# Two small projections of a token mixer from one matmul, with one part turned by an identity matmul and the other copied by DMA

## The chip, the core and the metric

The kernel runs on one core of one Trainium2 chip. A core has a matrix engine (PE, or TensorE), a vector engine (DVE), a scalar engine (ACT), a general engine (POOL, or GpSimd) and a queue engine (SP, or SyncE), and 16 DMA engines move data for it. The metric is the device time of one execution in microseconds (us), lower is better. Seven executions of the kernel before took 113.78 to 116.05 us, with a median of 114.7 us.

## The reference, cut to what matters

There are 4 batches, 8 heads, 768 tokens and 64 values per head; a head's 768 tokens are 8 blocks of 96. An 8x8 matrix P per head, made nearly doubly stochastic, mixes the blocks of k and of v. Attention then runs inside each block. Its output x (768 x 512 per batch) goes through a token mixer and a last matrix.

```python
k_sorted = einsum('bhij,bhjcd->bhicd', P, k_b);  v_sorted = einsum('bhij,bhjcd->bhicd', P, v_b)
attn = softmax(scale * q_b @ k_sb^T)          # inside each block of 96
x = attn @ v_sb                               # as (batch, 768, 512)
wq = x @ w_q;  wk = x @ w_k                   # 512 -> 64 each
W_tok = scale * einsum('bsd,btd->bst', wq, wk)
mixed = einsum('bst,btd->bsd', W_tok, x)
out = maximum(mixed, 0) @ w_out
```

The kernel computes mixed as wq times (wk transposed times x), so the 768 x 768 matrix is never made. For wk transposed times x it needs wk with tokens on partitions; for the product with wq it needs wq with its 64 values on partitions.

## The kernel before, in words

The program is a hand-written order of small units, the string ORDER (line 21). Each unit is named by kind, batch and number; a letter says which engine empties its PSUM tile (a for ACT, d for DVE), and a number after that asks for so many filler matmuls ahead of it (line 84: 256 columns of ones, which compute nothing that is used). Every engine works through its own instructions in this order. So PE does its matmuls exactly as ORDER lists them, and a unit whose data is late holds up all that stands behind it. The units, per batch:

- Q (line 202, 4 of them): q turned by identity matmuls. K (line 223, 4): k mixed by P and turned. V (line 237, 4): v mixed by P.
- T (line 247, 8): a DMA that regroups v by blocks, from VS to VT, on SP's queue; in batch 0 every second one goes on POOL's.
- S (line 255, 8): the scores of a block, then the exponential E on ACT. AV (line 269, 8): E times v, then reciprocal R and product X on DVE.
- XT (line 288, 4): two blocks of x turned, giving XT with the 512 features on partitions.
- WQ (line 300, 2): 4 matmuls over 384 tokens, giving wq transposed. The weight tile wqd holds w_q twice side by side, so that wq transposed stands on partitions 0 to 63 and again on 64 to 127.
- WK (line 310, 2): wk with tokens on partitions, 4 blocks with 4 accumulating matmuls each, so 16 matmuls of 64 columns. XT is the stationary operand.
- A (line 323, 1): wk transposed times x. MIX (line 336, 4): A times wq, with relu. The two halves of A stand on partitions 0 to 63 and 64 to 127, which is why wq is needed on both.
- OUT (line 353, 6): 4 matmuls of 512 columns with w_out, a copy on ACT or DVE, and a DMA to the output; for batch 3 on SP's queue, else on POOL's.

PSUM has 3 two-bank slots, in which K, V, S, AV and MIX take turns, and 2 one-bank slots, in which Q, XT, WQ, WK, A and OUT take turns. A unit waits until the unit that held its slot has been emptied.

The inputs are loaded by POOL's queue, in the order q0, v0, k0, q1 at the start, and then, in further_loads (line 180), after the regroups of batch 0: v1, w_q, w_k, k1, w_out, q2, v2, k2, q3, v3, k3. These DMAs turn fp32 into bf16. Between them POOL makes the mixing matrices M of batches 1 and 2 (line 217) and copies w_q into the second half of wqd (line 188), for which it waits until w_q has landed.

Of the kernel before, what the change touches and what calls it, by code (L numbers as in the profile page):

```python
# [10 lines left out]
FP32 = mybir.dt.float32  # L11
BF16 = mybir.dt.bfloat16
# [6 lines left out]


ORDER = """
    V00d3 V01a V02d V03a K01d K02a T00 K03a T04 K00d T03 T01 T02 T07 Q12d10 Q13a T06 S00a T05
    S01a S02a Q11d Q10d AV00d AV01d AV02d S03a S05a XT00d AV03d S04a S07a S06a AV04d XT01a V12d
    V11a AV07d WK00a WQ00a AV05d AV06d V13a K13a XT02d K11a K12d K10a XT03d V10a S13a1 S14a WQ01d
    T10 WK01d T12 S17a S12a T11 S11a A00d T14 T16 S16a Q23d Q21d T13 MIX02a MIX01d T17 Q20a Q22d
    T15 MIX03a MIX00d S10a OUT05a5 AV10d OUT02a AV11d AV12d AV14d OUT01a XT10a V20a V21d OUT03a
    V23a AV17d V22a OUT04d AV16d AV13d OUT00a T26 T25 K22a T24 K23d XT13a T22 S15a Q31d T23 K21a
    Q30d T21 K20d Q32a T27 AV15d XT11a T20 S24a2 S20a Q33d S21a WK10d V30d V33a WQ10a V31a AV24d
    V32a XT12d S22a AV21d T30 S23a WQ11a T32 AV22d AV20d T31 AV23d WK11a T35 K32a T36 A10a1 K30a
    K31d K33a T37 T33 T34 XT21d XT20a MIX13d MIX12a S34a WK20d3 WQ20a S31a S32a MIX11d OUT15d  # L30
    AV31d OUT13a AV32d OUT14a AV34d MIX10a S30a S33a S25a OUT10d OUT12a AV33d AV25d OUT11a AV30d
    XT31a S35a XT22d S26a XT30d1 S27a AV35d AV26d WK30a AV27d XT32a S36a WQ30d S37a XT23d AV36d
    AV37d2 WQ21a WK21a XT33d A20a WQ31a WK31d MIX20a MIX21d MIX22a A30a MIX23a OUT22a OUT21a
    MIX33d MIX30a MIX32a OUT25d OUT23a MIX31d OUT35a OUT34a OUT32a OUT30a OUT33a OUT31a OUT20a
    OUT24a
"""
SLOTS = {"b": 3, "s": 2}

# [2 lines left out]
def kernel(  # L41
# [22 lines left out]
    DH = moe_w_q.shape[1]  # L64
    PT = DM // P
# [16 lines left out]
    def filler(t):  # L82
        while fill[0] > 0:
            nc.tensor.matmul(t, idb, ones[:, 0:256], start=True, stop=True, skip_group_check=True)
            fill[0] -= 1

    def psum(shape, dtype=FP32):
        t = psp.tile(shape, dtype, tag="ps", name="ps", bufs=SLOTS["b"])
        filler(t[:, 0, 0:256])
        return t  # L90

    def psum1(n, dtype=FP32):
        t = psp.tile([P, 512], FP32, tag="ps1", name="ps1", bufs=SLOTS["s"])
        filler(t[:, 0:256])
        return (t if dtype == FP32 else t.bitcast(dtype))[:, 0:n]


    Pm = const.tile([BH, NB + 1, NB], FP32)
    nc.sync.dma_start(out=Pm[:, 0:NB, :], in_=sort_net.rearrange("b h i j -> (b h) i j"))

    Qn, Kn, Vn = [None] * B, [None] * B, [None] * B

    def load_q(b):
        Qn[b] = inp.tile([P, H, R6, D], BF16, tag="Qn", name="Qn", bufs=3)
        nc.gpsimd.dma_start(out=Qn[b].rearrange("p h r d -> p h (r d)"),
                            in_=q[b].rearrange("h (p r) d -> p h (r d)", p=P))

    def load_k(b):
# [11 lines left out]
    idb = const.tile([P, P], BF16)  # L120
# [48 lines left out]

    nc.gpsimd.tensor_copy(L_j, m_j.unsqueeze(2).to_broadcast([P, NB, SP]))  # L170
    load_q(1)
    wqd = const.tile([P, PT, 2, DH], BF16)
    wk_t = const.tile([P, PT, DH], BF16)
    wo_t = const.tile([P, PT, DM], BF16)
    nc.gpsimd.memset(VS[0][:, :, :, D:D1], 1.0)
    nc.gpsimd.memset(VS[1][:, :, :, D:D1], 1.0)
# [1 line left out]
        nc.gpsimd.memset(KTs[n][:, NP * S:], 0.0)  # L178

    def further_loads():  # L180
        load_v(1)
        make_m(1, PTR, nc.gpsimd)
        nc.gpsimd.dma_start(out=wqd[:, :, 0, :], in_=moe_w_q.rearrange("(t p) d -> p t d", p=P))
        nc.gpsimd.dma_start(out=wk_t, in_=moe_w_k.rearrange("(t p) d -> p t d", p=P))
        load_k(1)
        nc.gpsimd.dma_start(out=wo_t, in_=moe_w_out.rearrange("(t p) d -> p t d", p=P))
        load_q(2)
        nc.gpsimd.tensor_copy(wqd[:, :, 1, :], wqd[:, :, 0, :])
        make_m(2, PTR, nc.gpsimd)
        load_v(2)  # L190
        load_k(2)
        load_q(3)
        load_v(3)
        load_k(3)


    Xb, XT, QT, KT, VT, Ms, Es = {}, {}, {}, {}, {}, {}, {}
    wqT, wkb, Ab, mixT, ts = {}, {}, {}, {}, {}
    hf = S // 2
    copies = {"ACT": nc.scalar.copy, "DVE": nc.vector.tensor_copy}  # L200

# [11 lines left out]
    def make_m(b, src, eng, parts=1):  # L213
        M = rot.tile([P, H, SP, NB], BF16, tag="M", name="M", bufs=3)
        n = H // parts
        for h in range(0, H, n):
            eng.tensor_mul(  # L217
                M[:, h:h + n],
                src[:, b * H + h:b * H + h + n].unsqueeze(2).to_broadcast([P, n, SP, NB]),
                m_s.unsqueeze(1).unsqueeze(3).to_broadcast([P, n, SP, NB]))  # L220
        Ms[b] = M
# [76 lines left out]
        copies[eng](XT[b][:, :, 2 * j * BLK:(2 * j + 2) * BLK], ps)  # L298

    def u_WQ(b, h, eng):  # L300
        if b not in wqT:
            wqT[b] = rot.tile([P, S], BF16, tag="wqT", name="wqT")
        ps = psum1(hf)
        for pt in range(PT):
            nc.tensor.matmul(ps, wqd[:, pt].rearrange("p a d -> p (a d)"),
                             XT[b][:, pt, h * hf:(h + 1) * hf],
                             start=(pt == 0), stop=(pt == PT - 1), skip_group_check=True)
        copies[eng](wqT[b][:, h * hf:(h + 1) * hf], ps)

    def u_WK(b, h, eng):  # L310
        if b not in wkb:
            wkb[b] = rot.tile([BLK, NB, DH], BF16, tag="wkb", name="wkb")
        n = NB // 2
        ps = psum1(n * DH).rearrange("p (i d) -> p i d", i=n)
        for ii in range(n):
            i = h * n + ii
            m = P if ii < n - 1 else BLK
            for pt in range(PT):
                nc.tensor.matmul(ps[0:m, ii, :], XT[b][:, pt, i * BLK:i * BLK + m], wk_t[:, pt, :],
                                 start=(pt == 0), stop=(pt == PT - 1), skip_group_check=True)  # L320
        copies[eng](wkb[b][:, h * n:(h + 1) * n], ps[0:BLK])

    def u_A(b, n, eng):
        ps = psum1(DM // 2)
# [11 lines left out]
    def u_MIX(b, n, eng):  # L336
        if b not in mixT:
            mixT[b] = rot.tile([P, PT, R6, P], BF16, tag="mixT", name="mixT")
        wqv = wqT[b].rearrange("p (i r s) -> p r i s", i=NB, r=R6)
        rh, p2 = n // 2, n % 2  # L340
        nr = R6 // 2
        ps = psum([P, 2, 512])
        for a in range(2):
            nc.tensor.matmul(ps[:, a, 0:hf], Ab[b][a * DH:(a + 1) * DH, p2 * P:(p2 + 1) * P],  # L344
                             wqv[a * DH:(a + 1) * DH, rh * nr:(rh + 1) * nr],
                             start=True, stop=True, skip_group_check=True)
        ov = mixT[b].rearrange("p (a t) r n -> p a t (r n)", a=2)[:, :, p2, rh * hf:(rh + 1) * hf]
        if eng == "ACT":
            nc.scalar.activation(ov, ps[:, :, 0:hf], ACT.Relu)  # L349
        else:  # L350
            nc.vector.tensor_relu(ov, ps[:, :, 0:hf])  # L351
# [45 lines left out]


    emit = {"Q": u_Q, "K": u_K, "V": u_V, "T": u_T, "S": u_S, "AV": u_AV, "XT": u_XT,
            "WQ": u_WQ, "WK": u_WK, "A": u_A, "MIX": u_MIX, "OUT": u_OUT}  # L400
    for kind, b, n, eng, m in re.findall(r"([A-Z]+)(\d)(\d)([ad]?)(\d*)", ORDER):
        b, n, fill[0] = int(b), int(n), int(m or 0)
        if (kind, b, n) == ("S", 1, 0):
# [33 lines left out]
```

The softmax here doesn't subtract the row's maximum and nothing guards it: scores larger than these inputs give would overflow.

## Time and profile before

| what | value |
|---|---|
| median of 7 executions | 114.7 us (113.78 to 116.05) |
| the profiled execution's own time | 113.68 us |
| its span, first to last instruction | 111.9 us |
| mean granted PE clock | 0.969 of full speed |
| PE busy | 93.4 us (83%), 1444 matmuls |
| ACT, DVE, POOL busy | 75.5, 68.8, 33.4 us |
| DMA | 19.80 MB, mean 177 GB/s |

The busy time of an engine is a sum over stages that have different limits, so what bounds a stage is read from that stage. Matmuls are pipelined: the duration of one holds its latency, and what a unit really costs in a dense stretch is the time from its first matmul's start to the start of the next unit's. The profile's line numbers are those of the kernel before.

### The profile page before, as it was taken

How to read it: one execution, taken by the hardware profiler on the slowest of the kernel's cores; microseconds unless marked ns; L12 is line 12 of the kernel's file. 1: busy time of each engine (PE TensorE's matmuls, PEld its weight loads, DVE VectorE, ACT ScalarE, POOL GpSimd, SP SyncE). 2: the span in 40 equal slices, each digit the busy share in tenths (PEclk: the TensorE clock that was granted, in tenths of full speed). 3: DMA queues.
4: the chain of work that ended last, by engine and by line, in shares of the span. 5: the costliest groups of instructions: out<-in, count | busy, mean ns of one | idle time of the engine just before them, and what ended most of it. 6: DMA issues, size and time to landing. Idle time of an engine off the chain costs nothing.

```text
span 111.9 us, 3418 instructions
## 1 busy us (share of the span) xinstructions
PE 93.4 (83%) x1444; PEld 62.8 (56%) x1444; DVE 68.8 (62%) x154; ACT 75.5 (67%) x116; POOL 33.4 (30%) x54
## 2 busy tenths in 40 slices
PE   0007899978698999999999999999899999999930
PEld 0007345866575766666588688655478686334400
DVE  1686768579365734878898776858488874071000
ACT  4014538587836998849599986995968836885640
POOL 6950000999089910041310000003150000051030
PEclk9999999998559999999999999999999999999999
DMA  0999999789999999999999999602543000048772
GB/s 3 110 202 205 203 203 199 204 156 181 161 200 205 205 204 220 246 236 207 203 212 247 250 362 367 176 2 94 192 171 120 0 0 6 0 164 304 292 269 95
DMA packets 19758, 19.80 MB, mean 177 GB/s; under 512 B 2208, under 2 KB 17696, under 8 KB 19744
## 3 DMA queue, kind: packets, MB, share of 16 engines
q0 software_dynamic: 15696, 15.21, 72.9%
q1 hardware_dynamic: 4048, 4.38, 12.9%
q8 instruction: 11, 0.18, 0.6%
q14 instruction: 3, 0.02, 0.1%
HBM read 20.19 MB, written 6.29 MB: 237 GB/s over the span
## 4 chain that ended last, share of the span: by engine, by line
issue 41%; DMA 28%; POOL 14%; DVE 9%; PE 2%; ACT 1%; POOLq 1%; ACTq 0%
DMA Vn<-in_v_dram 22%; DMA wqd<-in_moe_w_q_dram 6%; POOL out_dram L362 5%; POOL Vn L115 2%; POOL M L217 2%; POOL VT L252 2%; DVE M L217 1%; DVE tmp L162 1%; DVE Pm L161 1%; ACT Pm L155 1%; DVE tmp L163 1%; DVE tmp L160 1%; DVE tmp L159 1%; PE ps L366 1%; DVE VS L244 1%
## 5 line engine op out<-in xcount | busy, mean ns | idle before, releaser
L362 POOL DMA_DIRECT2D out_dram<-ot x18 | 9.8, 546 | 59.3 <-ACT ot L360 35.1
L265 ACT ACTIVATE E<-ps 96x768 bf16<-96x768 f32 x32 | 24.0, 810 | 1.4 <-PE ps L260 1.3
L357 PE MATMUL ps<-wo_t,mixT 128*128 128x512 bf16 x96 | 23.1, 379 | 0.0
L284 DVE TENSOR_TENSOR X<-ps,R 96x512 bf16<-96x512 f32 x32 | 22.0, 686 | 1.1
L360 ACT COPY ot<-ps 128x512 f32<-128x512 f32 x20 | 11.8, 588 | 9.1 <-PE ps L357 9.0
L206 PE MATMUL ps<-idb,Qn 128*64 128x128 bf16 x192 | 8.9, 244 | 9.0 <-DMA Qn<-in_q_dram 8.7
L277 PEld LDWEIGHTS <-E 96*128 96x128 bf16 (+1 forms) x256 | 11.8, 104 | 4.9 <-ACT E L265 2.0
L277 PE MATMUL ps<-VT,E 96*128 96x65 bf16 (+1 forms) x256 | 13.3, 199 | 0.8 <-ACT E L265 0.7
L357 PEld LDWEIGHTS <-mixT 128*128 128x128 bf16 x96 | 8.6, 98 | 9.3 <-issue 0.9
L206 PEld LDWEIGHTS <-Qn 128*64 128x64 bf16 x192 | 7.0, 124 | 10.1 <-DMA Qn<-in_q_dram 8.7
L260 PE MATMUL ps<-QT,KT 64*128 64x96 bf16 x256 | 10.0, 210 | 1.4 <-DVE X L284 0.8
L244 ACT CAST VS<-ps 128x768 bf16<-128x768 f32 x11 | 8.8, 829 | 2.0 <-PE ps L241 2.0
L283 DVE RECIPROCAL R<-ps 96x8 f32<-96x8 f32 x32 | 6.3, 198 | 5.9 <-PE ps L277 5.8
L260 PEld LDWEIGHTS <-KT 64*128 64x128 bf16 x256 | 7.0, 97 | 4.5 <-issue 1.6
L351 DVE TENSOR_SCALAR mixT<-ps 128x768 bf16<-128x768 f32 x7 | 6.7, 954 | 4.0 <-PE ps L344 3.9
L241 PE MATMUL ps<-Vn,M 128*128 128x384 bf16 x32 | 8.4, 370 | 0.8 <-DMA Vn<-in_v_dram 0.8
L234 ACT CAST KT<-ps 128x768 bf16<-128x768 f32 x10 | 7.8, 800 | 1.1 <-PE ps L230 1.0
L294 PE MATMUL ps<-idb,X 96*128 96x96 bf16 x128 | 8.3, 211 | 0.0
L230 PE MATMUL ps<-M,Kn 128*64 128x128 bf16 x192 | 7.4, 220 | 1.0 <-DVE R L283 0.5
L349 ACT ACTIVATE mixT<-ps 128x768 bf16<-128x768 f32 x9 | 7.1, 815 | 0.5 <-PE ps L344 0.5
L230 PEld LDWEIGHTS <-Kn 128*64 128x64 bf16 x192 | 6.0, 109 | 2.6 <-issue 1.5
L211 ACT COPY QT<-ps 128x768 bf16<-128x768 bf16 x7 | 5.5, 793 | 2.8 <-PE ps L206 2.8
(71 smaller groups left out, 130.3 us busy)
## 6 DMA issues: line engine op xcount, KB each, us to landing
out_dram<-ot POOLq DMA_DIRECT2D x18, 256.0 KB, 2.6
Qn<-in_q_dram POOLq DMA_DIRECT2D x4, 768.0 KB, 14.5
Vn<-in_v_dram POOLq DMA_DIRECT2D x4, 768.0 KB, 11.9
Kn<-in_k_dram POOLq DMA_DIRECT2D x4, 768.0 KB, 14.8
VT<-VS SPq DMA_DIRECT2D x28, 97.5 KB, 5.5
out_dram<-ot SPq DMA_DIRECT2D x6, 256.0 KB, 2.0
wo_t<-in_moe_w_out_dram POOLq DMA_DIRECT2D x1, 512.0 KB, 11.3
VT<-VS POOLq DMA_DIRECT2D x4, 97.5 KB, 3.1
```

Source lines behind the costliest of these rows:

```text
L206: nc.tensor.matmul(ps[hh * D:(hh + 1) * D, r, :], Qn[b][:, 2 * kp + hh, r, :], idb, is_transpose=True, start=True, stop=True, skip_group_c ...
L230: nc.tensor.matmul(ps[hh * D:(hh + 1) * D, r * P:(r + 1) * P], Kn[b][:, h, r, :], Ms[b][:, h].rearrange("p s i -> p (s i)"), start=True, s ...
L241: nc.tensor.matmul(ps[:, hh, 0:R6 * D], Ms[b][:, h].rearrange("p s i -> p (s i)"), Vn[b][:, h].rearrange("p r d -> p (r d)"), start=True, ...
L244: copies[eng](VS[b % 2][:, :, 2 * kp:2 * kp + 2, 0:D].rearrange("p r h d -> p h r d"), ps[:, :, 0:R6 * D].rearrange("p h (r d) -> p h r d" ...
L260: nc.tensor.matmul(ps[:, hh, kp * BLK:(kp + 1) * BLK], KT[b][hh * D:(hh + 1) * D, k0:k0 + P], QT[b][hh * D:(hh + 1) * D, kp, :, i * SP:(i ...
L265: nc.scalar.activation(E.rearrange("p (a n) -> p a n", a=2), ps[0:BLK, :, 0:4 * BLK], ACT.Exp, scale=scale)
L277: nc.tensor.matmul(ps[0:m, h // 4, (h % 4) * D1:(h % 4 + 1) * D1], E[:, e * BLK:e * BLK + m], VT[b][:, i, h, :], start=True, stop=True, sk ...
L284: nc.vector.tensor_mul(Xb[b][:, i].rearrange("p (a t d) -> p a t d", a=2, t=4), pv[:, :, :, 0:D], Rt.unsqueeze(3).to_broadcast([BLK, 2, 4, ...
L294: nc.tensor.matmul(ps[:, pt, ii * BLK:(ii + 1) * BLK], Xb[b][:, 2 * j + ii, pt * P:(pt + 1) * P], idb[0:BLK, 0:BLK], is_transpose=True, st ...
L357: nc.tensor.matmul(ps, mixT[b][:, pt, r, :], wo_t[:, pt, :], start=(pt == 0), stop=(pt == PT - 1), skip_group_check=True)
L360: copies[eng](ot, ps)
L362: queue.dma_start(out=od[:, r, :], in_=ot)
```

## The change

One weight tile wkq now holds w_k and w_q side by side, so WQ's 4 matmuls give wk transposed on partitions 0 to 63 and wq transposed on 64 to 127 of one tile, wT. WK no longer multiplies by XT: it turns wT's k part with one identity matmul per block, 4 per unit instead of 16. The copy of wq on partitions 0 to 63, which MIX needs, is made by a new unit D, one DMA per batch on SP's queue from wT to the tile wq2. A new unit F only asks for a PSUM slot, so that fillers can stand at that place. The two weights are loaded as fp32 by SP's queue, behind SP's regroups of batch 0, and POOL turns them into bf16 with one copy in place of the copy that doubled w_q. ORDER is replaced as a whole. Beside D and F the number of units of each kind is the same; the number of fillers goes from 28 to 53.

```diff
-    V00d3 V01a V02d V03a K01d K02a T00 K03a T04 K00d T03 T01 T02 T07 Q12d10 Q13a T06 S00a T05
-    S01a S02a Q11d Q10d AV00d AV01d AV02d S03a S05a XT00d AV03d S04a S07a S06a AV04d XT01a V12d
-    V11a AV07d WK00a WQ00a AV05d AV06d V13a K13a XT02d K11a K12d K10a XT03d V10a S13a1 S14a WQ01d
-    T10 WK01d T12 S17a S12a T11 S11a A00d T14 T16 S16a Q23d Q21d T13 MIX02a MIX01d T17 Q20a Q22d
...
-    AV37d2 WQ21a WK21a XT33d A20a WQ31a WK31d MIX20a MIX21d MIX22a A30a MIX23a OUT22a OUT21a
-    MIX33d MIX30a MIX32a OUT25d OUT23a MIX31d OUT35a OUT34a OUT32a OUT30a OUT33a OUT31a OUT20a
-    OUT24a
+    V00d3 V01a V02d4 V03a K00d K01a K02a T05 T06 K03d T02 T03 T07 Q10d9 T01 Q12a T04 S06a S07a
+    S05a T00 Q13d Q11d AV06d F063 AV07d F073 AV05d S04a XT03d3 S03a AV04d S02a AV03d F032 S00a
+    S01a XT02d AV02d AV00d WQ01a AV01d V13a XT01a WK01d V12a V10d V11a XT00d T17 K10a7 K12d T12
+    K11a T14 WQ00a T15 K13a T10 WK00d3 D00 S14a4 S10a S13a T13 A00d T11 S17a1 T16 S16a4 S11a4
+    AV17d F172 S12a AV14d S15a AV12d Q22a1 Q23d MIX01a MIX00d MIX02a Q20d Q21a AV11d AV13d AV15d
...
+    AV21d XT23a V33a AV20d D10 A10a K32a K31d K30a T35 T37 XT20d T31 MIX13a MIX12d T34 MIX10a
...
+    S32a A20d S33a AV31d XT32a AV32d MIX21a AV33d WQ31a AV30d MIX20a WK31a XT31d MIX23a MIX22d
+    XT30a OUT22a WQ30a OUT24a WK30d D30 A30a OUT25a OUT20a MIX33d MIX30a MIX31a OUT23d OUT21a
+    MIX32d OUT31a OUT32a OUT34a OUT35a OUT33a OUT30a
...
+    wkq_f = const.tile([P, PT, 2, DH], FP32)
+    wkq = const.tile([P, PT, 2, DH], BF16)
...
     def further_loads():
+        for a, w in ((0, moe_w_k), (1, moe_w_q)):
+            nc.sync.dma_start(out=wkq_f[:, :, a, :], in_=w.rearrange("(t p) d -> p t d", p=P))
         load_v(1)
         make_m(1, PTR, nc.gpsimd)
-        nc.gpsimd.dma_start(out=wqd[:, :, 0, :], in_=moe_w_q.rearrange("(t p) d -> p t d", p=P))
-        nc.gpsimd.dma_start(out=wk_t, in_=moe_w_k.rearrange("(t p) d -> p t d", p=P))
         load_k(1)
         nc.gpsimd.dma_start(out=wo_t, in_=moe_w_out.rearrange("(t p) d -> p t d", p=P))
         load_q(2)
-        nc.gpsimd.tensor_copy(wqd[:, :, 1, :], wqd[:, :, 0, :])
+        nc.gpsimd.tensor_copy(wkq, wkq_f)
         make_m(2, PTR, nc.gpsimd)
...
     def u_WQ(b, h, eng):
...
         for pt in range(PT):
-            nc.tensor.matmul(ps, wqd[:, pt].rearrange("p a d -> p (a d)"),
+            nc.tensor.matmul(ps, wkq[:, pt].rearrange("p a d -> p (a d)"),
                              XT[b][:, pt, h * hf:(h + 1) * hf],
                              start=(pt == 0), stop=(pt == PT - 1), skip_group_check=True)
-        copies[eng](wqT[b][:, h * hf:(h + 1) * hf], ps)
+        copies[eng](wT[b][:, h * hf:(h + 1) * hf], ps)
+
+    def u_D(b, n, eng):
+        wq2[b] = rot.tile([DH, S], BF16, tag="wq2", name="wq2")
+        nc.sync.dma_start(out=wq2[b], in_=wT[b][DH:2 * DH, :])
 
     def u_WK(b, h, eng):
...
-            for pt in range(PT):
-                nc.tensor.matmul(ps[0:m, ii, :], XT[b][:, pt, i * BLK:i * BLK + m], wk_t[:, pt, :],
-                                 start=(pt == 0), stop=(pt == PT - 1), skip_group_check=True)
+            nc.tensor.matmul(ps[0:m, ii, :], wT[b][:, i * BLK:i * BLK + m], idb[:, 0:DH],
+                             start=True, stop=True, skip_group_check=True)
...
+    def u_F(b, n, eng):
+        psum1(512)
...
-        wqv = wqT[b].rearrange("p (i r s) -> p r i s", i=NB, r=R6)
+        wqs = [w.rearrange("p (i r s) -> p r i s", i=NB, r=R6) for w in (wq2[b], wT[b])]
...
-                             wqv[a * DH:(a + 1) * DH, rh * nr:(rh + 1) * nr],
+                             wqs[a][a * DH:(a + 1) * DH, rh * nr:(rh + 1) * nr],
```

More of the change, by code (lines that the diff above doesn't have):

```diff
@@ L21 @@
 ORDER = """
-    V00d3 V01a V02d V03a K01d K02a T00 K03a T04 K00d T03 T01 T02 T07 Q12d10 Q13a T06 S00a T05
-    S01a S02a Q11d Q10d AV00d AV01d AV02d S03a S05a XT00d AV03d S04a S07a S06a AV04d XT01a V12d
-    V11a AV07d WK00a WQ00a AV05d AV06d V13a K13a XT02d K11a K12d K10a XT03d V10a S13a1 S14a WQ01d
-    T10 WK01d T12 S17a S12a T11 S11a A00d T14 T16 S16a Q23d Q21d T13 MIX02a MIX01d T17 Q20a Q22d
-    T15 MIX03a MIX00d S10a OUT05a5 AV10d OUT02a AV11d AV12d AV14d OUT01a XT10a V20a V21d OUT03a
-    V23a AV17d V22a OUT04d AV16d AV13d OUT00a T26 T25 K22a T24 K23d XT13a T22 S15a Q31d T23 K21a
@@ L28 @@
[L28 to L32, printed above, removed]
-    AV37d2 WQ21a WK21a XT33d A20a WQ31a WK31d MIX20a MIX21d MIX22a A30a MIX23a OUT22a OUT21a
@@ new lines @@
+    OUT02a V20a OUT00a V23d XT11a V22a XT12d V21a AV16d OUT01a AV10d T22 K21a K23d T26 XT13a T27
+    K20a K22d T23 XT10a WQ11d T25 S21a T20 S20a S26a Q31d Q32d T24 T21 MIX03d Q30a Q33d S22a S27a
+    S23a WK11d WQ10d AV22d OUT04a AV27d AV23d WK10a AV26d OUT05a V30a OUT03a V31d V32a XT21d
+    AV21d XT23a V33a AV20d D10 A10a K32a K31d K30a T35 T37 XT20d T31 MIX13a MIX12d T34 MIX10a
+    WQ20a T33 MIX11d T30 S24a S25a OUT13d WK20a AV24d T36 T32 K33a AV25d OUT10a OUT14a S36a S37a
+    S35a XT22d OUT11d AV36d WQ21a AV37d OUT15a WK21d D20 AV35d S34a S31a XT33d OUT12a AV34d S30a
@@ L171 @@
     load_q(1)
-    wqd = const.tile([P, PT, 2, DH], BF16)
-    wk_t = const.tile([P, PT, DH], BF16)
     wo_t = const.tile([P, PT, DM], BF16)
@@ L197 @@
     Xb, XT, QT, KT, VT, Ms, Es = {}, {}, {}, {}, {}, {}, {}
-    wqT, wkb, Ab, mixT, ts = {}, {}, {}, {}, {}
+    wT, wq2, wkb, Ab, mixT, ts = {}, {}, {}, {}, {}, {}
     hf = S // 2
@@ L300, in u_WQ @@
     def u_WQ(b, h, eng):
-        if b not in wqT:
-            wqT[b] = rot.tile([P, S], BF16, tag="wqT", name="wqT")
+        if b not in wT:
+            wT[b] = rot.tile([P, S], BF16, tag="wT", name="wT")
         ps = psum1(hf)
         for pt in range(PT):
-            nc.tensor.matmul(ps, wqd[:, pt].rearrange("p a d -> p (a d)"),
+            nc.tensor.matmul(ps, wkq[:, pt].rearrange("p a d -> p (a d)"),
                              XT[b][:, pt, h * hf:(h + 1) * hf],
                              start=(pt == 0), stop=(pt == PT - 1), skip_group_check=True)
-        copies[eng](wqT[b][:, h * hf:(h + 1) * hf], ps)
+        copies[eng](wT[b][:, h * hf:(h + 1) * hf], ps)
+    def u_D(b, n, eng):
+        wq2[b] = rot.tile([DH, S], BF16, tag="wq2", name="wq2")
+        nc.sync.dma_start(out=wq2[b], in_=wT[b][DH:2 * DH, :])
     def u_WK(b, h, eng):
@@ L399 @@
     emit = {"Q": u_Q, "K": u_K, "V": u_V, "T": u_T, "S": u_S, "AV": u_AV, "XT": u_XT,
-            "WQ": u_WQ, "WK": u_WK, "A": u_A, "MIX": u_MIX, "OUT": u_OUT}
+            "WQ": u_WQ, "D": u_D, "F": u_F, "WK": u_WK, "A": u_A, "MIX": u_MIX, "OUT": u_OUT}
     for kind, b, n, eng, m in re.findall(r"([A-Z]+)(\d)(\d)([ad]?)(\d*)", ORDER):
```

## The prediction

> **What bounds the kernel now.** I read the page's busy times and slices, then PE's timeline, then the tiles of the loads and the stages around 30 us. First the page:
>
> ```profile
> PE 93.4 (83%) x1444; PEld 62.8 (56%) x1444; DVE 68.8 (62%) x154; ACT 75.5 (67%) x116; POOL 33.4 (30%) x54
> ...
> PEclk9999999998559999999999999999999999999999
> DMA  0999999789999999999999999602543000048772
> ```
>
> PE is the busiest, but two things differ over the span. A slice is 2.8 us. The DMA engines are at nine tenths until about slice 24 (67 us), so until then loads can set the pace. The granted PE clock is at half in slices 10 and 11. The chain that ended last runs mostly over POOL's queue of loads and stores and names no engine to shorten, so I went on to PE's timeline (start, duration, what, count):
>
> ```profile
> 35.77 0.44 PE L230 MATMUL ps<-M,Kn 128*64 128x128 bf16 x9 [0.51 <-DVE R L283]
> ...
> 67.54 0.53 PE L230 MATMUL ps<-M,Kn 128*64 128x128 bf16 x12
> ...
> 72.01 0.50 PE L84 MATMUL ps<-ones,idb 128*128 128x256 bf16 x3
> 72.37 0.70 PE L319 MATMUL ps<-wk_t,XT 128*128 128x64 bf16 x16
> 72.91 0.81 PE L305 MATMUL ps<-XT,wqd 128*128 128x384 bf16 x4
> ...
> 85.81 0.70 PE L319 MATMUL ps<-wk_t,XT 128*128 128x64 bf16 x16
> 86.34 0.44 PE L277 MATMUL ps<-VT,E 96*128 96x65 bf16 x8
> ...
> 100.17 7.11 PE L357 MATMUL ps<-wo_t,mixT 128*128 128x512 bf16 x32
> ```
>
> The first two rows are the first K matmuls of batch 1 and of batch 3. From start to next start a WK unit costs 0.53 us (85.81 to 86.34), a filler 0.12 (72.01 to 72.37, three). Read alike where PE goes from unit to unit without a gap: V 0.33, K and Q 0.34, S and AV 0.27, XT 0.37, WQ 0.66, A 0.90, MIX 0.20, OUT 0.865. The last PE work ends at 107.28; the remaining 4.6 us of the span are the last store and the end.
>
> The loads, from the answers for the tile of k, in the windows of k1's issue (25.70) and k3's (36.84):
>
> ```profile
> DMA to landing us min/median/max: 9.7/9.7/9.7
> ...
> DMA to landing us min/median/max: 30.1/30.1/30.1
> ```
>
> So k1 lands at 35.4 and k3 at 66.94, each just ahead of the first matmul that needs it (35.77, 67.54). The kernel has three parts: until 35.4 it waits for loads; from there to 67.5 PE does 28.9 us of units in 31.8, a factor of 1.10; from 67.5 to 107.28 it does 36.5 in 39.7, a factor of 1.09. From k1's arrival on PE is the bound, and before it PE work costs nothing while it fits:
>
> ```profile
> 24.00:28.00 4.00, 3.09 (x64) 2.46 (x65) 3.79 (x9) 2.90 (x5) 4.00 (x6) 0.86 1.18 167
> 28.00:32.00 4.00, 2.97 (x29) 1.95 (x29) 1.29 (x3) 2.41 (x4) 1.15 (x3) 0.50 1.47 171
> ```
>
> The columns are the stage, busy us with counts of PE, PE's weight loads, DVE, ACT and POOL, the granted clock, and DMA. PE is partly idle in both, and runs at half clock in the second.
>
> **The change part by part.** All sums are made against the profiled execution: 113.68 us, span 111.9. It is 1.0 us below the median of 114.7, so I take the difference in us over to the median.
>
> *WK.* 12 of 16 matmuls and weight loads per unit go; the 4 left have the same 64 columns. 0.53 x 4/16 = 0.13, so 0.40 less per unit. 7 of the 8 units stand behind k1's arrival in either order: -2.8. Bounds: -2.4 if an identity matmul costs half again as much, and -3.2 for all 8.
>
> Here a rule can be set beside the row. In the Trainium skill, "TensorE: Matmul & The Clock Gate", section "LDWEIGHTS (loading the stationary operand)", a weight load takes its columns over 1.2 ns, which would make 107 ns for 128 columns. The trace has 103 ns for one, yet 16 pairs of load and matmul pass in 0.53 us, 33 ns each, because they overlap. If loads were paid in series, by that page's figure the change would save 12 x 0.107 x 7 = 9.0 us; by the row it saves 2.8, and the row decides.
>
> *What moves ahead of k1.* I counted the units behind the first K unit of batch 1 in both orders. Before: 14 XT and 9 V; after: 12 XT and 8 V; all other kinds are equal but WK's cost. 2 x 0.37 + 0.33 = -1.1. This is free only if the first part still fits. After the change it holds 15.0 us of units and fillers between 15.48 and 35.4, 19.9 us, plus 7 fillers ahead of k1's matmuls that stand where PE waits. At half clock for as long as before (6.8 us) it would need 18.4. It fits; if it did not, up to 1.1 would come back.
>
> *Fillers.* 53 instead of 28, but behind k1's arrival 19 instead of 15: +0.5. The others lie under the wait for loads.
>
> These three make -3.4. Work in these parts has carried waits in proportion (factor 1.09), so -3.7.
>
> *Longer chain at the end.* WK now needs WQ's PSUM emptied first. In the last batch the order is XT30, OUT22, WQ30, OUT24, WK30, A30. Between WK30 and A30 nothing stands: 0.19 us latency and 0.42 of DVE's copy (line 321), with hand-overs about 0.7 us of idle PE. Between XT30 and WQ30 stands one OUT (0.865), against 0.80 of ACT's copy behind other ACT work: 0 to 0.6, I take 0.3. Sum +1.0, bounds +0.3 and +1.6. In the other batches two or more units stand between, at 0.
>
> *Scores of batch 1.* S14, S10, S13, S17, S16, S11, S12, S15 now come with only A, three AV and 16 fillers among them. ACT's exponential takes 0.74 each in a row, so 5.9 us against 5.6 of PE's units. +0.4, bounds 0 and 1.0.
>
> *The D copies.* Four DMAs of 96 KB on SP's queue, each waiting for both WQ copies of its batch. Behind D00 wait three regroups of batch 1, needed only by later AV units; behind D10 those of batch 3, which wait for v3 anyway; behind D30 the last stores, which come later. MIX waits for D. No trace shows this copy; the nearest rows are the regroups (97.5 KB, same queue), 5.2 to 7.2 us to landing at 39 to 45 us, 3.2 to 5.8 after 65 us. D00 is issued at about 38.5 and MIX01 comes up near 45: 0, bounds 0 and +0.7. D10 and D20 have about 10 us and are at 0. D30 has WK30, that idle 0.7, A30 and two OUTs ahead of MIX33, 3.5 us; SP's stores there land in 2.0, and I take 0, since DMA is nearly idle in the stage ahead of it; the upper bound is 5.8 - 3.5 = +2.3. Below zero nothing can come of a wait.
>
> *Loads and POOL.* POOL loses two issues (0.82 and 0.76 us) and the 2.85 us wait for w_q, and gets a copy of 512 elements from fp32 (the 256-element copy took 0.40; estimate 0.8). So k1 is issued 1.6 us earlier and v2 to k3 about 4 earlier. With DMA at nine tenths throughout, k1 stays behind v1 in the stream: 0, bounds -1.0 and +0.8. SP's fp32 loads are issued near 22 us; POOL's copy waits for them, and the loads from v2 on queue behind it, while k1, w_out and q2 keep the engines busy. Even the 6.9 us that w_q took to land leaves the copy done near 30.4, when WQ01 comes up. For k3: D00 and D10 add 0.19 MB, at 205 GB/s 0.9 us, so it lands near 67.9. PE does 30.1 us of units (7 waiting fillers left out) times 1.10 = 33.1 from 35.4 and is there at 68.5. So k3 is covered, by 0.6 us.
>
> Sum: -3.7 + 1.0 + 0.4 = **-2.3 us**; 111.4 for the profiled execution and 112.4 for the median. A second sum gives the same direction: ACT's units between k1 and k3 are 32.3 us against 30.2; if ACT set the pace there, k3's matmuls would start at 69.4, and 31.9 us of units x 1.09 + 1.0 behind them end at 105.2, 2.1 us before 107.28.
>
> **The rivals.** *All waits hidden.* The end chain and the scores cost their lower bounds and k1 comes 1.0 earlier: -3.7 + 0.3 - 1.0 = -4.4, 110.3 us. For it: k1 is issued earlier, and PE's fillers leave room. Against it: nothing stands between WK30 and A30.
>
> *The clock falls behind k1's arrival: slower.* By the stages the clock was at half from about 26.9 to 33.7 us, 6.8 us, after a stretch in which PE was busy 0.6 to 0.8 us of each us with no single idle over 0.3. The batch-1 scores are such a stretch, right after a wait for k1. Each us at half clock there costs 0.5; 6.8 us cost 3.4, which turns -2.3 into +1.1, 115.8. It decides from 4.6 us on. Against it stand 26 fillers around that stretch.
>
> A rule bears on this. The same page, Part 1, says that the clock halves only after an idle window of about 3.4 us. In this trace it fell without such idleness. By the rule this rival would be nearly excluded and its cost 0; by the row it stays, at up to 3.4.
>
> *The D copies come late: slower.* D00 at its upper end and D30 at 5.8 us plus an SP issue of 0.6: -2.3 + 0.7 + 2.9 = +1.3, 116.0. The point is D30 landing later than about 6 us after its issue. For it: the regroups of batch 1, under load, took 5.2 to 7.2. Against it: few transfers run there.
>
> *No change.* The removed WK work only turns into waits for ACT, which is busy nearly all of the middle part: the middle part ends as late as 70 and the chain costs 1.6, near 114.5.
>
> **How the numbers follow.** Forecast 42% (112.4, own range 111.2 to 113.6), all hidden 20%, clock 20%, D late 10%, no change 8%. Half a per cent (0.6 us) is about what this kernel's measurement can tell. Faster: 42 + 20 = 62%; same 8%; slower 20 + 10 = 30%. The range leaves out the outer tenth at each end: 109.8, half a us below "all hidden", to 116.2, just above "D late".
>
> **What the profile after would show.** WK units of 4 matmuls, 0.13 us to the next start; first K matmuls of batch 1 near 35.4 and of batch 3 near 68.5; about 35.8 us from there to the last OUT, ending near 105; an idle PE of 0.7 before A30, put down to DVE's wkb copy; MIX matmuls not waiting for the DMA of wq2. The prediction is wrong if PE reaches k3 later than 70, if the clock is at half behind 36 us, or if MIX waits for wq2.

## The result, and the profile after

The changed kernel is slower: 115.47 us median (114.94 to 117.15, 12 executions) against 114.69 us for the kernel before (31 executions). Here and below the medians are of all executions, while a ratio leaves out those that took over 1.5% longer than the fastest of the same kernel. The ratio is 1.012, with a 95% interval of 1.009 to 1.016, so the loss is small but clear. The forecast was 112.4 us, 2% faster. The profiled execution took 115.53 us with a span of 113.5, so 1.85 and 1.6 us more than the one of before.

The page of the changed kernel:

```profile
PE 93.4 (82%) x1373; PEld 62.3 (55%) x1373; DVE 67.9 (60%) x154; ACT 76.2 (67%) x116; POOL 32.1 (28%) x52
...
PEclk9999999999755599999999999999999999999997
DMA  0999999789999999999999984435544400325692
```

PE's busy time is the same as before: WK has 96 matmuls fewer, the fillers are 25 more, so 71 fewer in all. The sums hide what happened. A slice is 2.84 us. The clock is now at half for three slices and part of a fourth (about 30 to 40 us) instead of two and part of a third. DMA falls from nine tenths at slice 24 (68 us): k3 landed at 66.0, 8 us ahead of its first use, while before it landed 0.6 us ahead. PE's timeline of the changed kernel, with the idle time before a row and what ended it in brackets:

```profile
26.59 0.34 PE L260 MATMUL ps<-QT,KT 64*128 64x96 bf16 x8
29.04 0.43 PE L277 MATMUL ps<-VT,E 96*128 96x65 bf16 x8 [2.11 <-DMA VT<-VS]
...
35.26 1.46 PE L305 MATMUL ps<-XT,wkq 128*128 128x384 bf16 x4 [2.10 <-POOL wkq L188]
36.52 0.68 PE L277 MATMUL ps<-VT,E 96*128 96x65 bf16 x8
...
41.50 1.20 PE L230 MATMUL ps<-M,Kn 128*64 128x128 bf16 x36
...
74.07 1.17 PE L230 MATMUL ps<-M,Kn 128*64 128x128 bf16 x36
...
98.03 1.06 PE L333 MATMUL ps<-X,wkb 96*64 96x256 bf16 x16 [0.58 <-DVE wkb L324]
...
103.55 5.38 PE L363 MATMUL ps<-wo_t,mixT 128*128 128x512 bf16 x24
```

The row at 29.04 is AV04, and L305 at 35.26 is WQ01, the first use of the weights. The first K matmuls of batch 1 and batch 3 start at 41.50 and 74.07 (before: 35.77 and 67.54), and the last matmul ends at 103.55 + 5.38 = 108.93 (107.28). So from k of batch 1 to the end the change saves 71.5 - 67.4 = 4.1 us, more than was forecast. But that stretch begins 5.7 us later, although k1 had landed at 35.6 (issued at 24.5, 11.1 us to landing). 5.7 - 4.1 = 1.6 us, the whole difference of the spans. The time was lost ahead of k of batch 1, in the part where PE work was held to be free. There POOL's timeline shows its copy of the weights,

```profile
26.17 0.91 POOL L107 DMA_DIRECT2D Qn<-in_q_dram  x1
34.59 0.61 POOL L188 CAST wkq<-wkq_f 128x512 bf16<-128x512 f32 x1 [7.52 <-DMA wkq_f<-in_moe_w_q_dram]
```

and the answer for the fp32 tile shows its loads (count and duration of the issue, when it started, and the time to landing):

```profile
L182 SPq DMA_DIRECT2D wkq_f<-in_moe_w_k_dram x1: 596/596/596, 22.6 to 22.6; - x1
L182 SPq DMA_DIRECT2D wkq_f<-in_moe_w_q_dram x1: 559/559/559, 23.3 to 23.3; - x1
...
DMA to landing us min/median/max: 9.1/10.1/11.2
```

The second weight load landed 11.2 us after its issue, at 34.5; POOL waited 7.5 us for it, WQ01 waited for POOL, and everything behind WQ01 on PE waited too.

### The profile page after: what moved, and what is told of

It is laid out like the page before. It is cut to its first block, busy times and chain, and to the rows that moved or that the text cites. A ratio compares the mean times of both kernels' runs of the same rounds, so it can differ in the third digit from the quotient of the medians.

```text
span 113.5 us, 3288 instructions
## 1 busy us (share of the span) xinstructions
PE 93.4 (82%) x1373; PEld 62.3 (55%) x1373; DVE 67.9 (60%) x154; ACT 76.2 (67%) x116; POOL 32.1 (28%) x52
## 4 chain that ended last, share of the span: by engine, by line
PE 57%; DVE 10%; DMA 10%; ACT 9%; issue 4%; SPq 3%; POOL 2%; ACTq 0%; DVEq 0%; POOLq 0%
PE ps L363 19%; DMA wkq_f<-in_moe_w_q_dram 10%; PE ps L277 6%; PE ps L305 5%; PE ps L241 5%; ACT E L265 4%; PE ps L294 4%; PE ps L260 3%; PE ps L206 3%; SPq L252 3%; PE ps L230 3%; PE ps L350 3%; PE ps L333 3%; PE ps L84 2%; ACT KT L234 1%
## 5 line engine op out<-in xcount | busy, mean ns | idle before, releaser
L366 ACT COPY ot<-ps 128x512 f32<-128x512 f32 x21 | 12.3, 585 | 6.9 <-PE ps L363 6.9
L277 PE MATMUL ps<-VT,E 96*128 96x65 bf16 (+1 forms) x256 | 14.1, 201 | 2.6 <-DMA VT<-VS 2.1
L277 PEld LDWEIGHTS <-E 96*128 96x128 bf16 (+1 forms) x256 | 12.4, 106 | 6.1 <-issue 2.6
L84 PE MATMUL ps<-ones,idb 128*128 128x256 bf16 x53 | 8.9, 287 | 0.3 <-ACT PTR L402 0.3
L260 PE MATMUL ps<-QT,KT 64*128 64x96 bf16 x256 | 9.0, 208 | 0.0
L305 PE MATMUL ps<-XT,wkq 128*128 128x384 bf16 x32 | 7.2, 350 | 2.1 <-POOL wkq L188 2.1
L294 PE MATMUL ps<-idb,X 96*128 96x96 bf16 x128 | 8.8, 216 | 0.0
L211 ACT COPY QT<-ps 128x768 bf16<-128x768 bf16 x8 | 6.3, 796 | 2.8 <-PE ps L206 2.7
L260 PEld LDWEIGHTS <-KT 64*128 64x128 bf16 x256 | 6.5, 96 | 2.9 <-issue 1.9
L294 PEld LDWEIGHTS <-X 96*128 96x128 bf16 x128 | 7.1, 104 | 1.7 <-issue 0.7
## 6 DMA issues: line engine op xcount, KB each, us to landing
VT<-VS SPq DMA_DIRECT2D x28, 97.5 KB, 5.6
VT<-VS POOLq DMA_DIRECT2D x4, 97.5 KB, 3.4
```

What stands on the lines that cost most here:

```text
L260: nc.tensor.matmul(ps[:, hh, kp * BLK:(kp + 1) * BLK], KT[b][hh * D:(hh + 1) * D, k0:k0 + P], QT[b][hh * D:(hh + 1) * D, kp, :, i * SP:(i ...
L277: nc.tensor.matmul(ps[0:m, h // 4, (h % 4) * D1:(h % 4 + 1) * D1], E[:, e * BLK:e * BLK + m], VT[b][:, i, h, :], start=True, stop=True, sk ...
L294: nc.tensor.matmul(ps[:, pt, ii * BLK:(ii + 1) * BLK], Xb[b][:, 2 * j + ii, pt * P:(pt + 1) * P], idb[0:BLK, 0:BLK], is_transpose=True, st ...
L305: nc.tensor.matmul(ps, wkq[:, pt].rearrange("p a d -> p (a d)"), XT[b][:, pt, h * hf:(h + 1) * hf], start=(pt == 0), stop=(pt == PT - 1), ...
L366: copies[eng](ot, ps)
```

## The experiments

Two theories stood after this reading. *The late weights*: the place and kind of the weight loads set the start of k of batch 1. *A slow first part*: that part is late anyway, because the regroup T04 comes late (AV04 waited 2.1 us for it) and the clock falls.

**Weights by POOL's queue, as before the change (e1).** In e1, e2 and e3 the ORDER and all units are those of the change.

```diff
-        for a, w in ((0, moe_w_k), (1, moe_w_q)):
-            nc.sync.dma_start(out=wkq_f[:, :, a, :], in_=w.rearrange("(t p) d -> p t d", p=P))
         load_v(1)
         make_m(1, PTR, nc.gpsimd)
+        for a, w in ((0, moe_w_k), (1, moe_w_q)):
+            nc.gpsimd.dma_start(out=wkq[:, :, a, :], in_=w.rearrange("(t p) d -> p t d", p=P))
...
-        nc.gpsimd.tensor_copy(wkq, wkq_f)
```

> The changed kernel, but the two weights are loaded as before the change: by POOL's queue, turned into bf16 by the DMA, behind the mixing matrix of batch 1, with no copy on POOL. Theory (the late weights): in the changed kernel the fp32 weights, issued on SP's queue at 22.6 and 23.3 us, landed 9.1 and 11.2 us later, and POOL's copy, WQ01 and all of PE stood behind that; so here they land within 7 us of an issue near 25, WQ01 starts by 32.5 instead of 35.26, the first K matmul of batch 1 near 37 instead of 41.5, and the time is 111 to 113 us. Rival (the first part is slow anyway, by the clock at half and by the regroup that AV04 waits for): K of batch 1 still starts at 40 or later and the time is 114.5 to 116.

109.04 us, ratio to before 0.954 (0.941 to 0.967). The weights landed 7.0 and 6.6 us after their issue, WQ01 started at 32.07, k of batch 1 at 36.65, and the clock stayed full. WQ01 still waited 1.8 us for the weights. The time is 2 us below what the theory expected; the stretch behind k of batch 1 is better than was worked out from the old order's share of waits.

**Weights by POOL's queue, early (e2).**

```diff
     load_q(1)
+    for a, w in ((0, moe_w_k), (1, moe_w_q)):
+        nc.gpsimd.dma_start(out=wkq[:, :, a, :], in_=w.rearrange("(t p) d -> p t d", p=P))
...
-            nc.sync.dma_start(out=wkq_f[:, :, a, :], in_=w.rearrange("(t p) d -> p t d", p=P))
...
-        nc.gpsimd.tensor_copy(wkq, wkq_f)
```

> The changed kernel with the two weights loaded by POOL's queue as bf16 right behind q of batch 1, near 7 us, long before they are needed. Theory (the late weights): they land near 21 us, WQ01 never waits for them, v and k of batch 1 land as in the kernel before (near 31 and 36), K of batch 1 starts near 36.5, and the time is 110.5 to 112.5 us. Rival (slow first part anyway): K of batch 1 starts at 40 or later, 114.5 to 116 us.

108.71 us, ratio 0.955 (0.947 to 0.964), 1.8 us below the expected range. The weights landed near 21 us. PE's timeline of e2:

```profile
28.35 0.45 PE L275 MATMUL ps<-VT,E 96*128 96x65 bf16 x8 [0.25 <-ACT E L263]
30.66 0.81 PE L303 MATMUL ps<-XT,wkq 128*128 128x384 bf16 x4
31.30 0.44 PE L275 MATMUL ps<-VT,E 96*128 96x65 bf16 x8
...
35.24 1.20 PE L228 MATMUL ps<-M,Kn 128*64 128x128 bf16 x36
...
67.99 1.20 PE L228 MATMUL ps<-M,Kn 128*64 128x128 bf16 x36
...
97.50 5.38 PE L361 MATMUL ps<-wo_t,mixT 128*128 128x512 bf16 x24
```

WQ01 waits for nothing, k of batch 1 starts at 35.24, and from there to the end it takes 102.88 - 35.24 = 67.6 us, as in the changed kernel (67.4). So the two differ only ahead of k of batch 1, by 6.3 us: WQ01 starts 4.6 us later in the changed kernel, and from WQ01 to k takes it 6.2 us instead of 4.6. The second part goes with the clock, as the stages of the changed kernel show (busy us and counts of PE, weight loads, DVE, ACT, POOL, then the clock, DMA and GB/s),

```profile
28.00:32.00 4.00, 2.93 (x50) 2.31 (x51) 1.70 (x4) 1.62 (x3) 0.00 (x0) 0.74 1.28 194
32.00:36.00 4.00, 1.90 (x22) 1.43 (x21) 2.16 (x5) 0.69 (x1) 1.41 (x2) 0.50 1.29 204
36.00:40.00 4.00, 4.00 (x30) 2.57 (x29) 1.31 (x3) 2.60 (x4) 4.00 (x5) 0.50 1.29 205
```

beside those of e2:

```profile
28.00:32.00 4.00, 3.71 (x73) 2.81 (x68) 3.53 (x9) 2.98 (x5) 4.00 (x4) 1.00 1.31 203
32.00:36.00 4.00, 3.68 (x62) 2.70 (x62) 2.82 (x6) 3.12 (x5) 3.83 (x4) 1.00 1.28 206
36.00:40.00 4.00, 4.00 (x83) 3.01 (x77) 1.38 (x2) 3.46 (x6) 0.00 (x0) 1.00 1.26 197
```

These stages hold different units, so their counts can't be compared. But WQ01 itself, from its start to the next unit's, took 1.26 us at half clock (35.26 to 36.52) and 0.64 at full (30.66 to 31.30).

**Weights still by SP's queue, but first (e3).**

```diff
     wkq_f = const.tile([P, PT, 2, DH], FP32)
     wkq = const.tile([P, PT, 2, DH], BF16)
+    for a, w in ((0, moe_w_k), (1, moe_w_q)):
+        nc.sync.dma_start(out=wkq_f[:, :, a, :], in_=w.rearrange("(t p) d -> p t d", p=P))
```

(and the same loads taken out of further_loads)

> The changed kernel with its fp32 weight loads still on SP's queue, but as the first DMAs after sort_net, at about 1.2 us. If the place was wrong and not the queue: they land well before 27 us, POOL's copy does not wait, and the time is 111 to 113 us. If fp32 loads of short runs on SP's queue hurt the loads of POOL's queue wherever they stand: q and v of batch 0 land 2 us or more later, all that follows is later by as much, and the time is 113.5 us or more.

109.74 us, ratio 0.953 (0.940 to 0.966). The loads landed 2.3 and 5.2 us after their issue, POOL's copy did not wait, and k of batch 1 started at 36.08. The price is that PE waits 9.5 us instead of 8.6 for the first q. So fp32 and SP's queue are no fault in themselves; the place is.

**Longer runs at the same place (e4).** The rows of the weights belong to other features here.

```diff
-            nc.sync.dma_start(out=wkq_f[:, :, a, :], in_=w.rearrange("(t p) d -> p t d", p=P))
+            nc.sync.dma_start(out=wkq_f[:, 2 * a:2 * a + 2].rearrange("p t a d -> p (t a d)"), in_=w.rearrange("(p t) d -> p (t d)", p=P))
```

> The changed kernel with the weight loads at the same place on SP's queue, but each partition reads 4 neighbouring rows of a weight in one run of 1024 bytes in place of 4 runs of 256 bytes; the rows then belong to other features, so the output is not the reference's. If the short runs make the load slow beside POOL's stream: the landing falls from 9.1 and 11.2 us to below 6, WQ01 starts by 32, and the time is 111 to 113 us. If it is the queue's share that is small whatever the runs: landing at 9 us or more, time within half a per cent of the changed kernel's 115.5.

110.07 us, ratio 0.965 (0.956 to 0.974). The DMA view of e4:

```profile
wkq_f<-in_moe_w_k_dram SPq DMA_DIRECT2D x1, 128.0 KB, 7.5
wkq_f<-in_moe_w_q_dram SPq DMA_DIRECT2D x1, 128.0 KB, 7.6
```

The landing lies between the two expectations: 11.2 us became 7.6 when only the length of a run went from 256 to 1024 bytes. WQ01 started at 31.62 after 1.4 us of waiting, the clock stayed full, and k of batch 1 started at 36.21. The short runs are therefore a good part of the slowness, and they were decisive for the time; what remains is the wait among the other loads. The Trainium skill, "DMA: Bandwidth & Descriptors", section "Specifications", asks for at least 512 bytes per transfer for full rate. The measured 11.2 against 7.6 us agrees with it in direction.

**WK undone on top of e2 (e5).**

```diff
-            nc.tensor.matmul(ps[0:m, ii, :], wT[b][:, i * BLK:i * BLK + m], idb[:, 0:DH],
-                             start=True, stop=True, skip_group_check=True)
+            for pt in range(PT):
+                nc.tensor.matmul(ps[0:m, ii, :], XT[b][:, pt, i * BLK:i * BLK + m], wkq[:, pt, 0, :],
+                                 start=(pt == 0), stop=(pt == PT - 1), skip_group_check=True)
```

> The kernel with the weights loaded early by POOL's queue (108.7 us), with WK undone: again 16 matmuls of XT with w_k per unit in place of 4 identity matmuls of wT; the rest, the D copies too, as in the change. By the prediction's term for WK (0.40 us for each of 7 units behind k of batch 1): +2.8 us, so 111.3 to 111.9, and the stretch from the first K matmul of batch 1 to the end longer by 2.4 to 3.2 us. If WK's matmuls lie beside waits for ACT or DVE anyway: less than +1.0 us. The late wait of A30 for wkb becomes shorter either way.

110.45 us, ratio to before 0.963 (0.955 to 0.971). In PE's timeline of e5

```profile
34.73 1.20 PE L228 MATMUL ps<-M,Kn 128*64 128x128 bf16 x36
...
99.77 5.38 PE L362 MATMUL ps<-wo_t,mixT 128*128 128x512 bf16 x24
```

the stretch from k of batch 1 to the end is 105.15 - 34.73 = 70.4 us, against 67.6 in e2: +2.8, the term of the prediction. The time misses the expectation (111.3 to 111.9): the medians differ by only 1.7 us, the profiled executions by 2.1 (110.63 and 108.56). In this one k of batch 1 came 0.5 us sooner than in e2's; what makes up the rest isn't shown. The wait of A30 for wkb did not become shorter either: it is 0.58 us here too. So it comes from WK30 standing right ahead of A30 in the order, and not from the new way to compute wk.

**Early fillers taken out of e2 (e6).**

```diff
-    V00d3 V01a V02d4 V03a K00d K01a K02a T05 T06 K03d T02 T03 T07 Q10d9 T01 Q12a T04 S06a S07a
-    S05a T00 Q13d Q11d AV06d F063 AV07d F073 AV05d S04a XT03d3 S03a AV04d S02a AV03d F032 S00a
+    V00d3 V01a V02d V03a K00d K01a K02a T05 T06 K03d T02 T03 T07 Q10d9 T01 Q12a T04 S06a S07a
+    S05a T00 Q13d Q11d AV06d AV07d AV05d S04a XT03d S03a AV04d S02a AV03d S00a
```

> The kernel with the weights loaded early by POOL's queue (108.7 us) without the 15 fillers that the change put at V02, AV07, AV05, XT03 and S00, ahead of v of batch 1; the other 38 stay. If these fillers only stand under waits: the same time within half a per cent (108.2 to 109.2), clock or no clock. If they hold up the clock: it falls to half somewhere between 26 and 36 us, and K of batch 1 starts 1 to 3 us later, 109.5 to 111.5.

108.62 us, ratio 0.946 (0.937 to 0.955), the same median as e2 but a wider spread, 107.49 to 111.25. The profiled execution is the longest of the four; in it AV04 waited 1.72 us for its regroup, the clock fell to half just before 28 us, and k of batch 1 started at 38.03. The four executions took 107.49, 108.20, 109.03 and 111.25 us at a mean clock of 1.0, 0.998, 0.961 and 0.969. The two with a full clock are below all four of e2 (108.56 and more), so there the fillers give nothing and may cost some tenths. In e2, e9 and e10, which have these fillers, none of the 12 executions had a clock below 0.989. So they may also hold it up; four executions are too few to settle either.

**The early load in the kernel before (e7).**

```diff
     wqd = const.tile([P, PT, 2, DH], BF16)
     wk_t = const.tile([P, PT, DH], BF16)
+    nc.gpsimd.dma_start(out=wqd[:, :, 0, :], in_=moe_w_q.rearrange("(t p) d -> p t d", p=P))
+    nc.gpsimd.dma_start(out=wk_t, in_=moe_w_k.rearrange("(t p) d -> p t d", p=P))
```

(and the same loads taken out of further_loads)

> The kernel before the change, with only its two weight loads moved to right behind q of batch 1 on POOL's queue; order and matmuls as before. If the gain of the early load belongs to the changed order alone, which had put the weights' use behind a slow load: within 1% of the kernel before, 113.5 to 115 us. If late weights held back the kernel before as well: 3% or more faster, below 111.5.

114.02 us, ratio 0.997 (0.993 to 1.002). The early load is worth nothing in the old order; the 4.5% of e2 are the new units and order, once their weights are there. The trace suggests why. k1 landed at 34.39, sooner than before (35.4), yet its first matmul started at 36.02 (35.77). PE had waited for v1 (1.34 us, until 30.80) and then worked nearly without a gap. So in the old order it was not k1 that set the end of the first part, but v1 and the work behind it, part of it at half clock.

**The same loads by ACT's queue (e8).**

```diff
-            nc.sync.dma_start(out=wkq_f[:, :, a, :], in_=w.rearrange("(t p) d -> p t d", p=P))
+            nc.scalar.dma_start(out=wkq_f[:, :, a, :], in_=w.rearrange("(t p) d -> p t d", p=P))
```

> The changed kernel with its fp32 weight loads at the same place in the program, but issued by ACT's queue in place of SP's. If the regroup T04 landed late (6.9 us) because the weight loads stood right behind it on the same queue: T04 lands within 4 us, AV04 does not wait 2.1 us for it; the weights still land 7 us or more after their issue. If every DMA of that moment is slow: T04 stays at 5 us or more. Time between 110 and 115 us.

115.12 us (two executions, 113.79 and 116.46). The weights landed 9.4 and 11.7 us after their issue, as slowly as on SP's queue, and AV04 still waited, 3.2 us, for a regroup that took 7.6 us to land. The profiled execution is the longer of the two. So what makes the loads slow is not SP's queue alone, and the regroup can be late without the weights behind it on its queue; e6 shows that too.

**No D copies in e2 (e9).** Half of the mixed result uses the k part in place of wq.

```diff
-        wq2[b] = rot.tile([DH, S], BF16, tag="wq2", name="wq2")
-        nc.sync.dma_start(out=wq2[b], in_=wT[b][DH:2 * DH, :])
+        pass
...
-        wqs = [w.rearrange("p (i r s) -> p r i s", i=NB, r=R6) for w in (wq2[b], wT[b])]
+        wqs = [w.rearrange("p (i r s) -> p r i s", i=NB, r=R6) for w in (wT[b], wT[b])]
```

> The kernel with the weights loaded early by POOL's queue (108.7 us) without the four D copies: MIX reads its first half from the k part of wT, so wq is left out of half of the result. By the prediction the copies cost nothing: the same time within 0.6 us (108.1 to 109.3). If MIX's waits for them or their transfers matter: 1 us or more faster, below 107.7.

108.59 us against e2's 108.71: the copies cost nothing that can be measured, as expected.

**OUT25 ahead of A30 in e2 (e10).**

```diff
-    XT30a OUT22a WQ30a OUT24a WK30d D30 A30a OUT25a OUT20a MIX33d MIX30a MIX31a OUT23d OUT21a
+    XT30a OUT22a WQ30a OUT24a WK30d D30 OUT25a A30a OUT20a MIX33d MIX30a MIX31a OUT23d OUT21a
```

> The kernel with the weights loaded early by POOL's queue (108.7 us) with one unit moved in the last batch: OUT25 ahead of A30, so that PE has 0.87 us of work while DVE empties WK30. PE's idle time ahead of A30 was 0.7 us in the changed kernel and in this one. If it lies on the path to the end: 0.5 to 0.7 us faster, 108.0 to 108.2, and PE does not wait for wkb. If it is given back by a wait for A30's result at MIX33: the same time.

108.90 us against 108.71: no gain. The idle time ahead of A30 is gone, but PE's timeline of e10 has nearly the same wait one unit earlier:

```profile
91.76 1.02 PE L361 MATMUL ps<-wo_t,mixT 128*128 128x512 bf16 x4 [0.54 <-ACT ot L364]
92.71 1.06 PE L331 MATMUL ps<-X,wkb 96*64 96x256 bf16 x16
```

OUT25 needs one of the two one-bank PSUM slots, and WK30 and OUT24 hold both until ACT has emptied OUT24's. The wait was given back, not at MIX33 as the expectation had it, but by the slots.

**The regroup sooner in the changed kernel (e11).**

```diff
-    V00d3 V01a V02d4 V03a K00d K01a K02a T05 T06 K03d T02 T03 T07 Q10d9 T01 Q12a T04 S06a S07a
+    V00d3 V01a V02d4 V03a K00d K01a K02a T05 T06 K03d T04 T03 T07 Q10d9 T01 Q12a T02 S06a S07a
```

> The changed kernel, weights on SP's queue as in the change, with the regroups T04 and T02 of batch 0 exchanged, so that T04, for which AV04 waited 2.1 us, is SP's second. If the weights alone set the time: AV04 no longer waits, WQ01 still starts near 35, and the time stays at 114.5 to 116 us. If the late T04 and the clock that fell with it set it: K of batch 1 starts 2 us or more sooner and the time is below 113.5.

115.30 us, ratio 1.012 (1.005 to 1.020), as the changed kernel. PE's timeline of e11:

```profile
26.35 0.45 PE L277 MATMUL ps<-VT,E 96*128 96x65 bf16 x8
...
35.31 1.46 PE L305 MATMUL ps<-XT,wkq 128*128 128x384 bf16 x4 [5.61 <-POOL wkq L188]
...
41.16 1.20 PE L230 MATMUL ps<-M,Kn 128*64 128x128 bf16 x36
```

AV04 (26.35) no longer waits for its regroup, and WQ01 starts at the same time as before the exchange, after 5.6 us of waiting instead of 2.1. So the weights alone set the start of WQ01; the late regroup lay inside the wait for them.

**The loads alone in the kernel before (e12).**

```diff
+    wkq_f = const.tile([P, PT, 2, DH], FP32)
...
     def further_loads():
+        for a, w in ((0, moe_w_k), (1, moe_w_q)):
+            nc.sync.dma_start(out=wkq_f[:, :, a, :], in_=w.rearrange("(t p) d -> p t d", p=P))
...
-        nc.gpsimd.dma_start(out=wqd[:, :, 0, :], in_=moe_w_q.rearrange("(t p) d -> p t d", p=P))
-        nc.gpsimd.dma_start(out=wk_t, in_=moe_w_k.rearrange("(t p) d -> p t d", p=P))
...
-        nc.gpsimd.tensor_copy(wqd[:, :, 1, :], wqd[:, :, 0, :])
+        nc.gpsimd.tensor_copy(wk_t, wkq_f[:, :, 0, :])
+        for a in range(2):
+            nc.gpsimd.tensor_copy(wqd[:, :, a, :], wkq_f[:, :, 1, :])
```

> The kernel before the change with one part of the change alone: its weights as fp32 by SP's queue behind the regroups of batch 0, turned into bf16 by POOL at the place of the old copy; order and matmuls as before. If those loads land near 34 us here too: POOL's copies end near 35.5, WK00 and WQ00 start there in place of 32.5 and 33.4, and the time is 2 to 4 us longer than the kernel before's, 116.5 to 118.5. If they land by 30 us without the changed order: within 1 us of the kernel before.

117.32 us, ratio 1.021 (1.001 to 1.041). The loads landed after 9.2 and 11.5 us here too. But the first wait came at another place than expected. In PE's timeline of e12

```profile
33.85 1.44 PE L244 MATMUL ps<-Vn,M 128*128 128x384 bf16 x4 [4.37 <-DMA Vn<-in_v_dram]
```

the first V unit of batch 1 waited 4.4 us, while in the kernel before it waited 0.8. v1 landed 12.0 us after its issue instead of 9.2. This is the longest of the four executions (119.22 us), and in the changed kernel, with the same loads, v1 landed after 9.7 us. So it isn't shown that these loads delay v1. Nor does e12 show the weights alone holding up the old order: WK00 started at 35.56, behind that V, and POOL's last copy had ended at 35.06.

## Why the prediction was wrong, point by point

The step that failed is the one on loads and POOL, and in it this sentence: "Even the 6.9 us that w_q took to land leaves the copy done near 30.4, when WQ01 comes up." It took 6.9 us, which w_q had needed as bf16 in POOL's queue behind v1, as a bound for another kind of load, fp32 by SP's queue in competition with that stream. Measured: 11.2 us, copy done at 35.2. WQ01 did come up at 30.66 where its weights were there (e2), so the step had the moment of need right and the landing wrong. No row of the trace showed a load of that kind, so 6.9 was the nearest row and not an upper end, and the step named no price for the case that WQ01 has to wait. The same holds for "It fits" in the step on work moved ahead of k1: the units fit by their sum (15.0 us in 19.9), but the sum leaves out that one of them had not its operand until 35.2. The step on loads and POOL had one more thing wrong: v2 to k3 were to be issued about 4 us earlier, but POOL's wait of 7.5 us made it 3.7 later (v2 at 37.02 instead of 33.31). k3 landed in time even so. In e2 they were issued 3.9 us earlier.

- *WK*: right on the stretch from k of batch 1: -2.8 by the rows, 2.8 by e5. In the medians it is 1.7. A unit now takes 0.13 us to the next start (68.42 to 68.55).
- *Behind k of batch 1 in all*: better than forecast. Forecast 33.1 us to k of batch 3 and 35.8 from there to the last OUT; measured 32.6 and 34.9 (41.50, 74.07, 108.93), in e2 32.8 and 34.9.
- *Longer chain at the end*: 0.58 us of idle before A30 instead of 0.7, and 0.19 before WQ30 instead of 0.3. By e10 the first could only be moved; whether it is on the path to the end isn't shown. The bounds of +0.3 and +1.6 don't follow from the two parts, which give 0.7 and 1.3. The stretch from k of batch 1 is 1.5 us shorter than forecast; these two waits make up some 0.2 of that. The rest lies in the factor for waits, which was taken over from the old order: with the prediction's own unit costs it came out near 1.08 and 1.07, not 1.10 and 1.09.
- *Scores of batch 1*: the stretch took 6.7 us (44.31 to 50.97) for 5.8 us of units and fillers (the prediction has 5.6). With the factor of 1.09 the term of +0.4 gives 6.7. No run took it apart.
- *D copies*: right at 0, by e9. In the changed kernel D00 landed after 6.9 us, near its upper end, the others after 2.3 to 2.4, and MIX waited for one by 0.4 us at most (e3, e6, e11).
- *k3 covered*: right, but the wide margin in the changed kernel is luck: k3 landed at 40.56 + 25.4 = 66.0 and was first used at 74.07, because k of batch 1 had come late. In e2 it landed at 67.94, just ahead of its use at 67.99. So with the weights in time, the load of k3 is nearly the limit of the middle part.
- *Fillers*: e6 shows no loss or gain in the median from the 15 ahead of v of batch 1. The seven right ahead of k of batch 1, which the prediction left out as waiting, did not stand under a wait in the changed kernel: k1 had landed at 35.6, and they ran from 40.64 to 41.50. That is 0.86 us; no run took them out.
- *The signs of being wrong*: two of three came. PE reached k3 at 74.07, later than 70, and the clock was at half behind 36 us, until about 40. MIX did not wait for wq2 there.
- *The clock rival* came true in part. The clock was at half for about 10 us, but ahead of the first use of k1; it added some 1.7 of the 6.3 us there, and nothing behind. That the rival's 115.8 us lies near the 115.47 measured is chance: its cause was not the main one. In e2, without the wait, the clock stayed full, and in e11, with 5.6 us of it, it fell; but the kernel before lost it without such a wait, so waiting isn't the only cause.
- *The rule on the clock*, weighed in the prediction: by the Trainium skill, "TensorE: Matmul & The Clock Gate", "Part 1: The HAM clock gate", an idle window of about 3.4 us halves it. In the changed kernel it fell at about 30 us after one idle time of 2.1 us; in e4, with 1.4 us idle, and in e1, with 1.8 us, it stayed full. In e6 it fell 1.2 us into a wait. So here less idleness than the rule's was enough, and the rule would have priced that wait of 2.1 us without the slow matmuls that followed it.

## What to carry to other kernels

When a change moves a load to another queue, another type or another place in the stream, price its landing as unknown, however small it is: 256 KB of weights held up the whole kernel here, since an in-order engine stood behind their first use. Find the first use of every load moved, and what each microsecond of lateness costs there, before adding up what the change saves elsewhere. And when a change loses, take its parts away one by one: the matmuls and the order were worth 4.5%, and the place and form of one small load turned that into a loss of 1.2%.

## What the runs showed of the hardware that was not expected

- Small fp32 loads with 256-byte runs, issued by SP's or ACT's queue while POOL's queue streams, took 9.1 to 11.9 us to land (four kernels: the changed one, e8, e11, e12); with 1024-byte runs at the same place 7.5 and 7.6 (e4); first in the program, beside the first loads, 2.3 and 5.2 (e3); as bf16 by POOL's queue right behind v1 and M 6.6 and 7.0 (e1).
- The regroup T04, 97.5 KB on SP's queue at about 22 us, landed after 6.9 us in the changed kernel, 6.4 in e6 and 7.6 in e8, both without a load behind it on that queue, but after 2.9 to 3.4 in e1 to e4. The traces order these by the issue of v1 on POOL's queue. In the 14 profiled executions the last regroup of batch 0 on SP's queue landed after 2.8 to 4.6 us where it was issued ahead of v1 or at most 0.07 us behind it (ten executions), and after 5.3 to 7.6 where it was issued 0.18 us or more behind it (e6, e7, the changed kernel, e8). No run moved v1 or the regroup for this alone, so the cause is not shown.
